# A channel-quarter pipeline for the inverse transform of a fused attention and long-convolution kernel

## The chip, the cores and the metric

The kernel runs on one core of one Trainium2 chip. The metric is the device time of one execution in microseconds (us); the kernel before takes 2488.45 us in the median of three runs (2487.83 to 2496.6). Its profiled execution spans 2488.5 us, and all instants below are counted from the start of that span.

The engines are named as the profile names them: PE (matrix multiply, with PEld for its weight loads), DVE (vector), ACT (scalar/activation), POOL and SP. SP only issues transfers here. POOL computes a little and issues transfers too. Every engine works through its own instructions in a fixed order, so an instruction that waits holds up all that stand behind it on its engine.

## The reference

Two independent results are computed and laid side by side in the output.

Part A is an attention with a recurrent memory: for each of 64 segments of 32 rows, 8 memory rows are put in front, q, k and v are formed with 1024 x 4096 weights, a masked softmax attention over 40 positions and 32 heads is taken, and the output projection gives both the segment's rows and the next memory rows. Segment s+1 needs the memory of segment s.

Part B is a long convolution (S4). In short:

```
P  = exp(dt * (A_re + i A_im) * l)              # l = 0 .. 2047, for 1024 channels x 128 states
K  = real( sum_n  C * P * dt * B )              # a filter of 2048 taps for each of 1024 channels
y  = irfft( rfft(u, 4096) * rfft(K, 4096) )[:2048] + u * Dskip
```

## The kernel before, in words

Part B comes first and takes the span up to about 811 us; part A follows, with one pass of its loop for each segment. Part A reads its weights for each segment: 17 blocks of 512 KB are streamed from DRAM for every segment (the tiles `wst`), 45 blocks are kept in SBUF ("residents"), and two in PSUM. 34 of the residents are loaded while part B still runs, by the generator `residents` (line 1279), into space that part B gives back: 4 blocks into the tile tagged `kst`, 2 into `xTl`, 4 into `wsl`, and `EARLY = 24` (line 187) into a pool of their own. The other 11 are loaded on demand in the first segment (`unit`, line 244).

Part B has these stages.

- Parameters and the cosine/sine matrix `MF` (up to about 95 us).
- Tables (about 95 to 509 us): 16 steps `f`, each for 64 channels, plus a step before and one after. The order of work is a list of words written out by hand, `ORDER` (line 590). A word such as `E3` is an exponential on ACT, `K0'` a set of matrix products that yields filter values (tile `kp`), `x0'` its eviction by DVE into `KxT` (line 900). Every fourth step, `put_values` (line 909) makes 30 stores of `KxT` into the DRAM tensor `Kd`; they are kept in the list `late` and one is issued behind each exponential (line 1004), by POOL. Words with P, U and M advance three side works: P is part A's projections for rows known in advance (`projections`, line 106: slices of weights `wsl`, results evicted into `vst` or `kst` and stored to DRAM as `PVd` and `PKd`), U is the transform of the input u (`side`, line 837: matrix products `ups` over `u_h`, sums on DVE and POOL, stored to DRAM as `Ud`), M writes transposed 128-column pieces of `MF` to DRAM as `MId` (line 824).
- Two channel halves `dh` (509 to 745 us). For each half and each of 4 frequency blocks `kc`, `pointwise` (line 1126) makes twice: the spectrum of the filter by 32 products of 512 columns into two PSUM tiles `hps` (line 1137), a copy of the odd one by ACT (`osb_`), then ten vector instructions on DVE (lines 1150 to 1163) that multiply with u's spectrum (`uq`, loaded from `Ud`, line 959) into `Bt`. The negated filter rows `KN` (line 1121) are made by ACT.
- The inverse transform (`inverse`, line 1197): 16 products of 512 columns give 128 output rows of one half (`yp`); ACT copies them to `yb`, DVE adds u times Dskip (lines 1215, 1216) and POOL issues the store (line 1217). There are 16 pieces for each half. Those of half 0 run two at a time behind each spectrum of half 1, those of half 1 run at the end (745 to 811 us), each followed by the issue of two residents from ACT's queue. Each piece first loads its matrix `mi` (256 KB, `MId`) and `uu` (a piece of u), three pieces ahead (`NIV = 3`, line 1166).

What a line can't say is the order in the last loops:

```
    for dh in range(2):
...
        for kc in range(4):
            pointwise(dh, kc, ks[dh], Bt)      # in it, after each spectrum: inverses(2 if dh == 1 else 0)
...
    for c in range(16):
        inverses(1)
        for _ in range(2):
            next(resident, None)
```

Of the kernel before, what the change touches and what calls it, by code (L numbers as in the profile page):

```python
# [64 lines left out]
class Ahead:  # L65
# [40 lines left out]
    def projections(self):  # L106
# [29 lines left out]
        for i, (m, t, c) in enumerate(slices):  # L136
# [3 lines left out]
            for j in range(2):  # L140
                a = take([128, 512], F32, "pro")
                if m == "v":
# [5 lines left out]
                    def evict(copy, a=a, t=t, c=c, j=j):  # L148
                        if late:
                            late.pop(0)()  # L150
                        vst = vals.tile([128, 2, 2, 128], BF16, name="vst", tag="vst", bufs=3)
                        copy(out=vst[:].rearrange("p b h e -> p (b h e)"), in_=a[:])
                        nc.sync.dma_start(out=self.PVd[t][:].rearrange("(b p) f -> p b f", p=128)[:, 2 * j:2 * j + 2, 256 * c:256 * c + 256],
                                          in_=vst[:].rearrange("p b h e -> p b (h e)"))
                        counted("v", t, 16, lambda: rows_out(t))
                else:
# [4 lines left out]
                    def evict(copy, a=a, m=m, t=t, g=g, h=h2 + j, mo=mo):  # L161
                        if late:
                            late.pop(0)()
# [23 lines left out]
EARLY = 24  # L187
# [409 lines left out]
def part_b(ctx, tc, u, A_re, A_im, B_re, B_im, C_re, C_im, log_dt, Dskip, out_b, ahead, copies, residents):  # L597
# [22 lines left out]
    ctx_m = ctx.enter_context(ExitStack())  # L620
    mfp = ctx_m.enter_context(tc.tile_pool(name="b_mf", bufs=1, side="right"))
    MF = mfp.tile([128, 16, 2, 512], BF16, name="MF")
# [182 lines left out]

    tmp = ctx1.enter_context(tc.tile_pool(name="b_tmp", bufs=2))
    up = ctx1.enter_context(tc.tile_pool(name="b_up", bufs=1, side="right"))
    ps_t = ctx1.enter_context(tc.tile_pool(name="b_pst", bufs=2, space=PSUM))
    ps_e = ctx1.enter_context(tc.tile_pool(name="b_pse", bufs=1, space=PSUM))
# [4 lines left out]
    def load_uh(dh):  # L814
        t_ = up.tile([128, 16, DH], BF16, name="u_h", tag="u_h")
        for r in range(4):
            sy.dma_start(out=t_[:, 4 * r:4 * r + 4, :], in_=u_r[r][:, :, DH * dh:DH * dh + DH])
        return t_[:].rearrange("p c (t s e) -> p c s t e", t=4, e=8)

# [17 lines left out]
    def side():  # L837

        for dq in range(4):
            if dq % 2 == 0:  # L840
                uv = load_uh(dq // 2)
            for kc in range(4):
                got = {}
                for r in (0, 2, 1, 3):
                    ps = take([128, 2, DQ], F32, "ups")
                    for cs in range(2):
                        for mc in range(4):
                            pe.matmul(ps[:, cs, :], lhsT=MF[:, 4 * r + mc, cs, 128 * kc:128 * kc + 128], rhs=uv[:, 4 * r + mc, 8 * (dq % 2):8 * (dq % 2) + 8],  # L848
# [25 lines left out]
    def load_par(sb):  # L874

        for q in range(2):
            for h in range(2):
                gp.dma_start(out=par_t[sb % 2][q][24 * h:24 * h + 24],
                             in_=PB[q][:].rearrange("c (d t) (g h s e) n -> d g s h c t e n", d=2, g=2, h=2, s=4)[sb // 8][sb // 4 % 2][sb % 4][h])
# [16 lines left out]
    def part_out(sb, t, kp):  # L896
        if sb % 4 == 0 and t == 0:
            KxT["t"] = tmp.tile([128, NC, 128], BF16, name="KxT", tag="KxT")
# [7 lines left out]
    def put(out, in_):  # L906
        late.append(lambda eng=gp: eng.dma_start(out=out, in_=in_))
# [51 lines left out]
    def load_u(dh, kc):  # L959
        us = {}  # L960
        for q in (0, 2, 1, 3):
            us[q] = ahead.pool.tile([128, 2, 2, DQ], F32, name="uq", tag="wsl", bufs=4)
            sy.dma_start(out=us[q][:].rearrange("p a c d -> p a (c d)"), in_=Ud[kc, 2 * dh:2 * dh + 2, :, q].rearrange("a p c d -> p a (c d)"))
        return us

# [18 lines left out]
    def phase_matmul(r, e):  # L986
        r, e = (r, e) if e else (r + 1, 0)
        pt = T["t", r, e] = ps_t.tile([128, 8 * NT], F32, name="ptt", tag="ptt")
        pe.matmul(pt[:], lhsT=pars[r][1][:, e, :], rhs=RT[:].rearrange("p a b -> p (a b)"), start=True, stop=True)
# [17 lines left out]
    def shifted(r, e):  # L1007
        kM = T["k", r, e] = tmp.tile([128, 8 * NT], F32, name="kM", tag="kM")
        sc.activation(out=kM[:], in_=T["t", r, e][:], func=ACT.Identity, bias=magic[:])

    def turns(r, e):
# [3 lines left out]
        v.scalar_tensor_tensor(out=T["n", r, e // 4][:, lo:lo + 8 * NT], in0=T.pop(("k", r, e))[:], scalar=MAGIC, in1=T.pop(("t", r, e))[:],  # L1015
# [58 lines left out]
    for f in range(-1, 17):  # L1074
# [6 lines left out]
        if f == 16:  # L1081
            while ahead.late:
                ahead.late.pop(0)()
            spectra = [load_u(0, 0)]
        for word in ORDER:
            nm, r = word.rstrip("'"), f - word.endswith("'")
            if nm in evict_of:
# [10 lines left out]
    for n_, f_ in enumerate(late):  # L1098
        f_((sy, gp)[n_ % 2])
    for g in (bg, mb):  # L1100
# [9 lines left out]
    ctx3 = ctx.enter_context(ExitStack())  # L1110
    ivs = [ctx3.enter_context(tc.tile_pool(name="b_iv", bufs=2))]
    ctx2 = ctx.enter_context(ExitStack())
    ktp = ctx2.enter_context(tc.tile_pool(name="b_KT", bufs=1))
    bp0 = ctx2.enter_context(tc.tile_pool(name="b_B0", bufs=1))
    pw = ctx2.enter_context(tc.tile_pool(name="b_pw", bufs=1))
    ps_h = ctx.enter_context(tc.tile_pool(name="b_psh", bufs=3, space=PSUM))
    ps_y = ctx.enter_context(tc.tile_pool(name="b_psy", bufs=2, space=PSUM))
    out_v = out_b.rearrange("(c p r) d -> r c p d", p=128, r=4)
    u_v = u.rearrange("(c p r) d -> r c p d", p=128, r=4)

    def negate(KT):
        KN = ahead.pool.tile([128, 8, DH], BF16, name="KN", tag="xTl")
        sc.activation(out=KN[:], in_=KT[:, 8:16, :], func=ACT.Copy, scale=-1.0)
        return KN

    def pointwise(dh, kc, KT, Bt):
        us = spectra.pop(0)
        for half in range(2):

            s_ = []  # L1130
            for r in range(2):
                ps = ps_h.tile([128, 2, DH], F32, name="hps", tag="h")
                for cs in range(2):
                    for i, rr in enumerate((r, r + 2)):
                        for mc in range(4):
                            rhs = KNs[dh][:, 4 * (rr - 2) + mc, :] if half == 1 and i == 1 else KT[:, 4 * rr + mc, :]
                            pe.matmul(ps[:, cs, :], lhsT=MF[:, 4 * rr + mc, cs, 128 * kc:128 * kc + 128], rhs=rhs,  # L1137
                                      start=(i == 0 and mc == 0), stop=(i == 1 and mc == 3))
                s_.append(ps)
            o_ = pw.tile([128, 2, DH], F32, name="osb_", tag="o")  # L1140
            if half == 0:
                sc.copy(out=o_[:], in_=s_[1][:])
            else:
                sc.copy(out=o_[:, 0, :], in_=s_[1][:, 1, :])
                sc.activation(out=o_[:, 1, :], in_=s_[1][:, 0, :], func=ACT.Copy, scale=-1.0)
            if len(KNs) == dh:
                KNs.append(negate(KT))
            qs = (0, 2) if half == 0 else (3, 1)
            X = pw.tile([128, 2, 2, DH], F32, name="x", tag="x")
            v.tensor_tensor(out=X[:, 0], in0=s_[0][:], in1=o_[:], op=ALU.add)  # L1150
            v.tensor_tensor(out=X[:, 1], in0=s_[0][:], in1=o_[:], op=ALU.subtract)  # L1151
            Y = pw.tile([128, 2, 2, DH], F32, name="y", tag="y")
            split = "p c (a d) -> p c a d"
            for n_, q in enumerate(qs):
                uc, un = (us[q][:, :, i, :].unsqueeze(1).to_broadcast([128, 2, 2, DQ]) for i in range(2))
                x_ = X[:, n_].rearrange(split, a=2)
                v.tensor_tensor(out=Y[:, n_].rearrange(split, a=2), in0=uc, in1=x_, op=ALU.mult)
                v.tensor_tensor(out=x_, in0=un, in1=x_, op=ALU.mult)
            v.tensor_tensor(out=Y[:, :, 0, :], in0=Y[:, :, 0, :], in1=X[:, :, 1, :], op=ALU.subtract)
            v.tensor_tensor(out=Y[:, :, 1, :], in0=Y[:, :, 1, :], in1=X[:, :, 0, :], op=ALU.add)  # L1160
            first = 0 if half == 0 else 1
            for j, op in ((0, ALU.add), (1, ALU.subtract)):
                v.tensor_tensor(out=Bt[:, kc, half, j], in0=Y[:, first], in1=Y[:, 1 - first], op=op)
            inverses(2 if dh == 1 else 0)

    NIV = 3

    def load_inverse(dh, c):
        r, mc = c // 4, c % 4
        iv = ivs[-1]  # L1170
        mi = iv.tile([128, 2, 4, 128], BF16, name="mi", tag="mi", bufs=NIV)
        sy.dma_start(out=mi[:], in_=MId[c])
        uu = iv.tile([128, 512], BF16, name="uu", tag="uu", bufs=NIV + 1)
        sy.dma_start(out=uu[:], in_=u_v[r, mc][:, DH * dh:DH * dh + DH])
        return mi, uu

    def negated(c, mi):
        neg = (None, (1, 2), (0, 2), (0, 1))[c // 4]
        mn = None
        if neg:  # L1180
            mn = ivs[-1].tile([128, 2, 4, 128], BF16, name="mn", tag="mn", bufs=2)
            sc.activation(out=mn[:, neg[0]:neg[1]], in_=mi[:, neg[0]:neg[1]], func=ACT.Copy, scale=-1.0)
# [4 lines left out]
    def inverses(n):  # L1187

        for _ in range(n):
            dh_, c = todo.pop(0)  # L1190
            if not ready:
                ready.append(negated(c, nxt[0][0]))
            inverse(dh_, Bs[dh_], c, *nxt.pop(0), *ready.pop(0))
# [3 lines left out]
    def inverse(dh, Bt, c, mi, uu, neg, mn):  # L1197
        r, mc = c // 4, c % 4
        iv = ivs[-1]
        yp = ps_y.tile([128, DH], F32, name="yp", tag="yp")  # L1200
        j = r % 2
        n = 0
        for kc in range(4):
# [133 lines left out]
```

## Time and profile before

| stretch (us) | what runs | PE busy | DVE busy | transfers |
|---|---|---|---|---|
| 450 to 500 | last tables | 35.07 of 50 | 44.86 of 50 | 174 GB/s |
| 500 to 550 | end of tables, half 0 | 39.10 | 36.33 | 190 GB/s |
| 550 to 600 | half 0 | 34.20 | 49.38 | 111 GB/s |
| 600 to 650 | half 0 ends, half 1 | 35.09 | 44.41 | 123 GB/s |
| 650 to 700 | half 1 with inverses | 49.09 | 40.70 | 148 GB/s |
| 700 to 750 | the same | 37.02 | 38.20 | 163 GB/s |
| 750 to 800 | last inverses, residents | 40.70 | 8.84 | 344 GB/s |
| 859 to 1300 | part A, steady | 373.10 of 441 | 232.41 of 441 | 378 GB/s |

In the profile, an engine's busy time counts instructions that compute, not those that issue transfers; PE's is a union of overlapping, pipelined products. A line of the waits reads: who waited, for whom, the total in us, how often, and the longest. In a line of a stretch the engines stand in the order PE, PEld, DVE, ACT, POOL, each with its busy time and its number of instructions, followed by PE's granted clock, the share of the transfer engines and GB/s. On the timeline a line has start, duration, engine, line, operation, output and inputs, shape, and in brackets the engine's idle time before it with what ended it.

### The profile page before, as it was taken

To read this page: it belongs to the slowest core of one execution; us is meant where nothing else is said; L and a number is where in the kernel's file an instruction comes from. 1 tells how busy PE (TensorE), PEld (TensorE's weight loads), DVE (VectorE), ACT (ScalarE), POOL (GpSimd) and SP (SyncE) were. 2 spreads that over 40 slices of the span, in tenths; PEclk is the share of its full clock that TensorE was granted. 3 is DMA by queue.
4 is the path that set the end of the run, shared out by engine and by line. 5 is a ranking of instruction groups with operands and counts; after the bars stand their busy time and mean duration, and the time that the engine had idled before them with its cause. 6 is when DMAs were issued, how large, how long until landed. Compare 5 with 4: busy or idle time off the path is not lost.

```text
span 2488.5 us, 76343 instructions
## 1 busy us (share of the span) xinstructions
PE 2017.4 (81%) x32774; PEld 1085.3 (44%) x32774; DVE 1471.0 (59%) x3159; ACT 965.1 (39%) x1543; POOL 351.7 (14%) x629
## 2 busy tenths in 40 slices
PE   1689788775978688888888888878888888888889
PEld 1356565532433244444444444444444444444444
DVE  9589788879781354545455555545555454545450
ACT  6689788911212233233333232323332323232321
POOL 2235556540001000000000000000000000000020
PEclk9799999988999799999999999999999999999999
DMA  6685964554349999999999999999999999999992
GB/s 160 180 229 157 268 185 141 157 178 138 109 153 344 358 385 383 366 378 374 378 383 387 376 389 380 385 370 351 369 388 357 386 364 383 367 383 372 382 393 81
DMA packets 383273, 763.17 MB, mean 307 GB/s; under 512 B 119462, under 2 KB 211590, under 8 KB 380886
## 3 DMA queue, kind: packets, MB, share of 16 engines
q1 hardware_dynamic: 363094, 700.46, 78.1%
q0 software_dynamic: 14928, 39.99, 4.8%
q10 hardware_dynamic: 4912, 17.84, 2.1%
q8 instruction: 256, 4.19, 0.7%
q14 instruction: 83, 0.68, 0.1%
HBM read 703.35 MB, written 67.88 MB: 310 GB/s over the span
## 4 chain that ended last, share of the span: by engine, by line
DMA 35%; PE 29%; DVE 17%; issue 10%; ACT 6%; SPq 1%; POOL 1%; DVEq 0%; ACTq 0%; POOLq 0%
DMA wst<-WD_k 16%; PE acc L339 11%; DMA wst<-WD_o 10%; PE pp L438 3%; DMA wst<-WD_v 3%; PE pe L561 2%; PE pro L158 2%; PE ups L848 2%; DVE nr L1026 2%; PE tr L350 2%; PE yp L1209 1%; DMA PVd<-vst 1%; PE pa L995 1%; DVE piece L278 1%; DMA mi<-MId 1%
## 5 line engine op out<-in xcount | busy, mean ns | idle before, releaser
L339 PEld LDWEIGHTS <-hT 128*32 128x32 bf16 x12352 | 328.1, 97 | 467.2 <-issue 247.0
L339 PE MATMUL acc<-wst,hT 128*32 128x512 bf16 x3072 | 313.3, 392 | 161.4 <-DMA wst<-WD_k 65.2
L345 ACT CAST ev<-acc 128x512 bf16<-128x512 f32 x384 | 224.7, 585 | 409.5 <-PE acc L339 404.7
L438 PEld LDWEIGHTS <-oT 128*32 128x32 bf16 x8192 | 204.2, 97 | 118.4 <-issue 92.0
L278 DVE TENSOR_SCALAR piece<-keep 128x256 int32<-128x256 int32 (+1 forms) x640 | 191.0, 363 | 53.4 <-PE pp L438 29.9
L438 PE MATMUL pp<-W_o,oT 128*32 128x256 bf16 x5120 | 211.7, 276 | 7.2 <-DMA W_o<-in_A_Wo_dram 7.2
L339 PE MATMUL acc<-W_v,hT 128*32 128x512 bf16 x3072 | 210.9, 379 | 0.0
L339 PE MATMUL acc<-W,hT 128*32 128x512 bf16 x2560 | 205.9, 393 | 0.0
L377 DVE TENSOR_REDUCE mx<-sc 128x8 f32<-128x320 f32 x128 | 62.4, 488 | 242.4 <-PE sc L370 242.2
L351 DVE COPY KT<-tr 128x512 bf16<-128x512 bf16 x64 | 27.2, 425 | 266.1 <-PE tr L350 266.1
L438 PE MATMUL pp<-wst,oT 128*32 128x256 bf16 x2560 | 128.9, 278 | 41.8 <-DMA wst<-WD_o 32.6
L358 POOL COPY KT<-pk 128x128 bf16<-128x128 bf16 x128 | 37.6, 294 | 812.2 <-PE sc L370 446.6
L351 ACT COPY QT<-tr 128x512 bf16<-128x512 bf16 x128 | 74.9, 585 | 188.5 <-PE tr L350 188.5
L1209 PE MATMUL yp<-Bt,mi 128*128 128x512 bf16 x384 | 113.3, 403 | 36.4 <-DMA mi<-MId 27.6
L425 ACT CAST oT<-pv 128x512 bf16<-128x512 f32 x128 | 75.0, 586 | 168.8 <-PE pv L411 164.7
L339 PE MATMUL acc<-W_q,hT 128*32 128x512 bf16 x1792 | 134.0, 379 | 0.0
L312 POOL COPY hT<-xt 128x192 bf16<-128x192 bf16 x64 | 22.2, 347 | 722.1 <-DMA xt<-XTd 404.7
L158 PE MATMUL pro<-xTl,wsl 128*128 128x512 bf16 x512 | 119.7, 385 | 5.2 <-ACT xTl L102 5.2
L379 ACT ACTIVATE sc<-sc 128x320 f32<-128x320 f32 x128 | 54.0, 422 | 153.8 <-DVE sc L378 150.7
L1137 PE MATMUL hps<-KT,MF 128*128 128x512 bf16 x384 | 94.1, 395 | 18.0 <-DVE x L1151 17.4
L339 PE MATMUL acc<-W_k,hT 128*32 128x512 bf16 x1536 | 108.5, 389 | 0.0
L350 PE MATMUL tr<-a_ident,ev 128*128 128x128 bf16 x1024 | 102.2, 223 | 0.8 <-ACT KT L351 0.7
(280 smaller groups left out, 3637.7 us busy)
## 6 DMA issues: line engine op xcount, KB each, us to landing
wst<-WD_o SPq DMA_DIRECT2D x320, 512.0 KB
wst<-WD_k SPq DMA_DIRECT2D x256, 512.0 KB
wst<-WD_q SPq DMA_DIRECT2D x256, 512.0 KB
wst<-WD_v SPq DMA_DIRECT2D x256, 512.0 KB
Ud<-ux POOLq DMA_DIRECT2D x16, 1024.0 KB, 5.6
uq<-Ud SPq DMA_DIRECT2D x32, 512.0 KB
pk<-PKd SPq DMA_DIRECT2D x64, 192.0 KB
wsl<-in_A_Wk_dram SPq DMA_DIRECT2D x16, 512.0 KB
```

The source lines that it names most:

```text
L158: nc.tensor.matmul(a[:], lhsT=w[:, kc, 128 * j:128 * j + 128], rhs=xTl[:, kc, :, :].rearrange("p s k -> p (s k)"), start=(kc == 0), stop=( ...
L278: nc.vector.tensor_scalar(out=out.bitcast(I32), in0=in_.bitcast(I32), scalar1=0, scalar2=None, op0=ALU.bitwise_or)
L339: nc.tensor.matmul(a[32 * g:32 * g + 32, o_:o_ + rhs.shape[1]], lhsT=hT[:, kc, :], rhs=rhs, start=(kc == 0), stop=(kc == KC - 1), tile_pos ...
L345: nc.scalar.copy(out=q[:], in_=a[:])
L350: nc.tensor.transpose(out=p[:, i, hl, :, :].rearrange("p a b -> p (a b)"), in_=q[:, 128 * hl:128 * hl + 128], identity=ident[:])
L351: eng(out=dst, in_=p[:, i, :, :, :])
L377: nc.vector.tensor_reduce(out=mx[:], in_=sc, axis=AX.X, op=ALU.max)
L379: nc.scalar.activation(out=sc, in_=sc, func=ACT.Exp, scale=scale)
L425: nc.scalar.copy(out=o[:], in_=p[:].rearrange("p a (g q) -> p a g q", g=4))
L438: nc.tensor.matmul(po[32 * qt:32 * qt + 32, :], lhsT=oT[:, h % 4, (h % 16) // 4, :], rhs=columns(w, 1024 * hh + 256 * qt, 256)[0][1], star ...
L1137: pe.matmul(ps[:, cs, :], lhsT=MF[:, 4 * rr + mc, cs, 128 * kc:128 * kc + 128], rhs=rhs, start=(i == 0 and mc == 0), stop=(i == 1 and mc = ...
L1209: pe.matmul(yp[:], lhsT=m_[:, cs, kc, :], rhs=Bt[:, kc, half, j, c_, :], start=(n == 0), stop=(n == 15))
```

## The change: four channel quarters in one pipeline

The transform is cut into 16 blocks: four channel quarters of 256 channels, four frequency blocks each. A block's spectrum covers both halves of the complex result at once (64 products of 256 columns), and is issued one block ahead of its pointwise part, so that the next spectrum stands on PE before the inverses. From block 4 on, each block is followed by two inverse groups of the previous quarter (a group is two pieces of 128 rows, 32 products of 256 columns), and 8 groups are left for the end. The inverse matrices are loaded once and kept in SBUF (`MI`, 32 KB for each partition) instead of being read for each half. The first block's spectrum goes into the PSUM tiles of the tables' own pools and is issued at the start of the tables' last step; its `KN` is made by POOL at the end of the step before that. The order of the channels in the tables is changed to fit (`load_par`).

Around it: the 30 stores of each `put_values` are issued by SP instead of POOL; two stores of the list `late` of the projections, not one, go with each eviction, and `vst` has 6 buffers, not 3; `u_h` is loaded in quarters into two buffers, the second and third well ahead; the last such stores (`PKd` from `PVd`) are issued after the filter stores; `uu` comes through POOL's queue, in one transfer for two pieces; the residents are issued by SP, in other places (3 at block 0, 4 at block 6, 8 at block 14 into the space of `MF`, 19 with the last inverses).

```diff
-                        if late:
+                        for _ in range(min(2, len(late))):
                             late.pop(0)()
-                        vst = vals.tile([128, 2, 2, 128], BF16, name="vst", tag="vst", bufs=3)
+                        vst = vals.tile([128, 2, 2, 128], BF16, name="vst", tag="vst", bufs=6)
...
-EARLY = 24
+EARLY = (3, 13)
...
-    def load_uh(dh):
-        t_ = up.tile([128, 16, DH], BF16, name="u_h", tag="u_h")
+    def load_uq(dq):
+        t_ = up.tile([128, 16, DQ], BF16, name="u_h", tag="u_h%d" % (dq % 2))
...
     def put(out, in_):
-        late.append(lambda eng=gp: eng.dma_start(out=out, in_=in_))
+        late.append(lambda eng=sy: eng.dma_start(out=out, in_=in_))
...
         if f == 16:
-            while ahead.late:
-                ahead.late.pop(0)()
-            spectra = [load_u(0, 0)]
+            spectra = [load_u(0), load_u(1)]
         for word in ORDER:
+            if f == 15 and word == "u0":
+                negate(ks[0], gp)
+            if f == 16 and word == ORDER[0]:
...
+                spectrum(0, first)
...
     for n_, f_ in enumerate(late):
         f_((sy, gp)[n_ % 2])
+    while ahead.late:
+        ahead.late.pop(0)()
...
+    for b in range(16):
...
+        if b == 0:
+            ks.append(load_k(1, (gp,), ktp.tile([128, 16, DH], BF16, name="KT", tag="KT")))
+            for _ in range(EARLY[0]):
+                next(resident)
+        if b == 3:
+            nxt = [load_inverse(*todo[n_]) for n_ in range(NIV)]
+            pointwise(b, *now)
...
+        if b + 1 < 16:
+            s_ = [ps_h.tile([128, 2, 2, DQ], F32, name="hps", tag="h") for _ in range(2)]
+            spectrum(b + 1, [halves(t_) for t_ in s_])
+            then = s_[0][:], odd([halves(t_) for t_ in s_])
+        if b == 6:
+            negate(ks[1])
+            for _ in range(4):
+                next(resident)
+        if b == 14:
+            for _ in range(8):
+                next(resident)
+        if b != 3:
+            pointwise(b, *now)
+        now = then
+        if b + 2 < 16:
+            spectra.append(load_u(b + 2))
+        if b < 4:
+            sy.dma_start(out=MI[:, 4 * b:4 * b + 4], in_=MId[4 * b:4 * b + 4].rearrange("c p a k q -> p c a k q"))
+        if b >= 4:
+            inverses(2)
     ctx2.close()
-    ctx_m.close()
-    for c in range(16):
+    for _ in range(8):
         inverses(1)
-        for _ in range(2):
+        for _ in range(3):
             next(resident, None)
```

## The prediction

> **What bounds the kernel now.** I read the slices of the span first. Part A (right of the 14th slice) has its transfers at 0.9 or more throughout; the stretches in the table above give 378 GB/s at share 1.00 there. The change leaves its 17 streamed blocks per segment alone, so what part A takes after its first segment (859 to 2488 us) stays. All that can move is part B.
>
> ```profile
> ## 2 busy tenths in 40 slices
> PE   1689788775978688888888888878888888888889
> DVE  9589788879781354545455555545555454545450
> ACT  6689788911212233233333232323332323232321
> ...
> DMA  6685964554349999999999999999999999999992
> ```
>
> Each digit stands for 62.2 us. In slices 3 to 8, most of the tables, DVE and ACT are both at 0.7 to 0.9. Then DVE alone is high, then PE, then transfers: three stages that follow one another with one busy engine each. That is what a pipeline could fold together. Next the waits of three stretches. Tables, 95 to 512 us:
>
> ```profile
> ACT vst L152 <- DMA PVd<-vst: 12.8, 4, 4.5
> DVE kst L167 <- DMA PVd<-vst: 8.7, 2, 4.6
> ACT kst L167 <- DMA PVd<-vst: 4.5, 2, 2.6
> PEld L848 <- DMA u_h<-in_B_u_dram: 2.2, 1, 2.2
> ```
>
> ACT and DVE stop for a store of `vst` to land, since only three buffers exist. How much this costs I read from the timeline: the first of each step's two DVE instructions of line 1026 that the chain lists comes 23.0 us after that of the step before in undisturbed steps, but steps that evict `vst` or change `u_h` take 26 to 29. Summed over the steps from 120.86 to 497.16 us, the excess over 23.0 us is 31.5 us.
>
> Half 0 and half 1:
>
> ```profile
> DVE x L1150 <- DMA Kd<-KxT: 10.7, 1, 10.7
> ...
> PE hps L1137 <- DVE x L1151: 17.4, 5, 4.8
> ```
>
> ```profile
> ACT yb L1214 <- PE yp L1209: 47.3, 20, 11.1
> DVE uu L1216 <- ACT yb L1214: 42.6, 14, 4.9
> ...
> PE yp L1209 <- DMA mi<-MId: 27.6, 7, 14.9
> ```
>
> DVE idles 10.7 us between its last table eviction (509.37) and the first `x` (520.07), because PE, ACT and DVE start the first spectrum only then; the named store is merely the last of several releasers. Until 616 us PE waits for DVE and no inverse runs. At the end PE waits for `mi` while residents fill the queues. So 509.4 to 811.0 us (DVE's last add, 810.58 + 0.42), 301.6 us, is the stretch to rework.
>
> [...] the trace has 1214 to 1226. The new pointwise keeps ten instructions of 1024 elements per partition, so it must cost the same. [...] 8 products `ups` of 256 columns take 1.03 us, (1.03 - 0.27)/7 = 0.109 us each, weight loads hidden. [...] The trace shows what issue costs: 18 filter stores on SP took 13.71 us (0.76 each), on POOL 8 took 4.53 (0.57).
>
> **The change, part by part.**
>
> Tables. More `vst` buffers, two `late` stores per eviction and `u_h` in two buffers aim at the 31.5 us. Six evictions fit a 23 us step, so a buffer comes round after a whole step; the `vst` waits seen were under 5 us beyond three buffers, so they go. Not all the excess need go: `kst` still has one buffer. Against it, 90 filter stores of the first three quarters move to SP inside the tables: 90 x 0.76 = 68 us of issue over 370 us, in front of `wsl` loads that are issued three slices (one step) ahead. SP has gaps (it issues nothing from 163 to 172 us, for one), so I count this as hidden. Bounds 0 and -31; I take -20.
>
> POOL's `KN`. 4096 bf16 per partition; from POOL's copies of 128 and 192 elements (294, 347 ns) 0.83 ns per element, 3.6 us in all. Behind it stand the last `ux` sums (7.2 us) and `Ud` store, needed only by the last quarter. `KT` has been loaded by 491 + 2 us, so `KN` is ready by about 498, and the first spectrum (64 x 0.109 = 7.0 us) ends by 502, before the last `kp` products (505.7). ACT is free from 500.7. Hence DVE starts the first `x` right after its last table cast: -10.7.
>
> Blocks 0 to 3. DVE: 11.85 us per block (532.69 to 544.54, one old half-block without a gap), 47.4 in all. PE needs 7 of each 12. One new wait: SP has 15 filter stores (11.5 us), 8 `PKd` stores (8 x 1.33 from 10.68 for 8), `Dsk` and three residents in front of the load for block 2. That is issued about 25 us after the tables' end, and behind 1.6 MB of residents and scattered stores lands at about 34, while DVE wants it at 26: +8 (0 to 15). Nothing else stands behind it but DVE itself.
>
> Blocks 4 to 15. DVE: 11.85 + 4 adds of u in 1.90 (645.16 to 647.06) = 13.75. PE: 64 + 64 products x 0.109 = 13.95. ACT: odd copies, `yb`, negated matrices, under 7. With the spectrum one block ahead, PE and DVE need not wait for each other within a block: the even tile of block b is freed by DVE's `x` two spectra later. So 11 blocks at 13.9 (153), the last pointwise 11.85, then 8 groups x 3.49 = 27.9 and 1.5 to evict: 194. `KN` for the second half (3.62 us on ACT) and `MI` (4.2 MB, once, where 8.4 MB were read) lie beside DVE's work.
>
> Sum: 47.4 + 8 + 194 = 250 us from the tables' end, against 301.6: -52, the 10.7 included.
>
> Hand-over. The residents no longer have 66 us of tail. 8 can go once the last spectrum is done, 12 groups (42 us) before the end, 19 more by the end: 27 x 0.524 = 14.2 MB, with u and the outputs 17.3 MB, at 344 to 378 GB/s 46 to 50 us, so 4 to 8 us late. The two blocks for PSUM, formerly fetched at 732 us, now wait for space until the inverses are over: before, PE resumed 8.6 us after its last inverse; a chain of store, load, copy and load makes about 12. The two overlap in part: +5 (0 to 12). The first segment then loads its 28 blocks as before (811 to 859).
>
> Total: 2488.5 - 20 - 52 + 5 = 2421.5, say 2422.
>
> **Rivals.**
>
> - Tables gain nothing: SP's new work eats what the buffers give. For it: SP holds to its order, and waits up to 10.9 us for `vst` producers in single cases. Against: POOL loses as much. 2488.5 - 52 + 5 = 2441.
> - PE and DVE in lockstep from block 4: if the next spectrum had to wait for this block's `x`, a block would be x 2.45 + the rest of the spectrum 5.2 + inverses 7.0 + ACT 0.75 + DVE 0.43 = 15.8; 11 x 1.9 = 21 more: 2443. For it: three double-bank PSUM tiles serve two per block. Against: the odd tile is free as soon as ACT has copied it.
> - Everything better: -31 in the tables, no stall at block 2 (-60 in place of -52), no late loads: 2488.5 - 31 - 60 = 2397.5. For it: PE's tail leaves slack that I gave to neither. Against: the residents' 46 us of transfers in 42.
> - Slower: SP becomes the bound of the tables, and the 68 us of issue lie on the path, with the rest as forecast: 2488.5 + 68 - 52 + 5 = 2509. For it: part A's projections depend on SP's loads. Against: issue is idle for whole stretches.
>
> **How the numbers follow.** Forecast 0.52, tables gain nothing 0.20, lockstep 0.13, better 0.09, slower 0.06. Range: 2398 to 2460. The low end is the better case. The high end is no gain in the tables (+20), a stall 7 us longer and a hand-over 7 us later together (2456), or lockstep with one of these (2450). Outside are the slower case, part of the better one and lockstep without the tables' gain (2463): about 2 in 10. Faster by over 0.5% (under 2476): 0.93; within: 0.03; slower: 0.04.
>
> **What would show it.** Tables: waits for `PVd` gone, steps of 23 us, end near 490. Start: first `x` within 1 us of the last table cast. Blocks: `x` every 12, then every 14 us; a wait of DVE for `uq` at block 2. PE at 9 tenths from block 4 on. `mi` waits gone. First segment's PE about 10 to 14 us after the last inverse. Part A's steady part unchanged at 1629 us. Wrong it would be if SP's queue holds up `wsl`, if blocks take 16 us, or if the residents are later than 10 us.

## The result, and the profile after

The changed kernel takes 2430.78 us (median of 4 runs, 2426.8 to 2432.11) against 2488.14 us before on the same chip (4 runs, 2483.58 to 2496.6). The ratio is 0.9763, with a 95% interval from 0.9734 to 0.9792. The forecast was 2422 us within 2398 to 2460. The profiled execution spans 2428.7 us, 59.8 us less than before.

Cut at instants that both timelines show, the 59.8 us are made up as follows (a step begins at DVE's first sign-bit clearing, line 1026 before, 1050 after; the tables end with the last cast into `KxT`; the transform ends with DVE's last addition to `uu`; the third segment of part A is dated by its copy of `KT`, line 351).

| stretch | before (us) | after (us) | difference | forecast |
|---|---|---|---|---|
| to the start of the tables' last step | 494.87 | 462.51 | -32.4 | |
| last step, to the tables' end | 14.5 | 25.1 | +10.6 | both: -20 |
| tables' end to the transform's end | 301.6 | 254.7 | -46.9 | -52 |
| transform's end to the third segment | 77.0 | 85.0 | +8.0 | +5 |
| the rest of part A | 1600.5 | 1601.4 | +0.9 | 0 |

The slices of the span come first, as before; a digit now stands for 60.7 us.

```profile
PE   1699999669996888888888888888888888888879
...
DVE  9599999989972445455554545454545545454540
ACT  6699999603332233232333333332323233332321
...
DMA  6686974583368999999999999999999999999992
```

PE, DVE and ACT stand together at 9 in slices 3 to 7, where before they changed between 7 and 9. In slices 10 to 12 PE and DVE are high at once (9, 9, 9 and 9, 9, 7), where before DVE was high first and PE later. Between the two, in slices 8 and 9 (425 to 546 us), PE has 6: there the last step and the first blocks lie. A table of stretches says the same in busy time: the columns are the ends of the stretch, its length, the busy time of PE, PEld, DVE, ACT and POOL (with counts), PE's granted clock, the share of the transfer engines and GB/s.

```profile
500.00:550.00 50.00, 31.29 (x233) 25.37 (x234) 40.43 (x36) 3.41 (x9) 19.27 (x34) 0.76 0.90 292
550.00:600.00 50.00, 47.06 (x432) 41.89 (x431) 44.74 (x47) 19.76 (x33) 8.68 (x12) 1.00 0.45 158
600.00:650.00 50.00, 50.00 (x461) 44.79 (x459) 47.12 (x52) 14.65 (x29) 11.56 (x16) 1.00 0.32 107
650.00:700.00 50.00, 50.00 (x461) 44.77 (x459) 47.66 (x50) 16.55 (x32) 8.67 (x12) 1.00 0.39 131
```

From 600 to 700 us PE is busy for the whole of both stretches and DVE for 47 of 50: the pipeline is bound by PE, one block each 13.97 us. What is lost against the forecast up to the transform's end lies before 600 us. Three of the waits between 455 and 545 us name most of it (who waited, for whom, total, times, longest):

```profile
...
ACT nr L1053 <- DVE nr L1050: 9.5, 2, 7.9
...
DVE y L1167 <- DMA uq<-Ud: 7.6, 1, 7.6
PE pa L989 <- POOL KN L974: 6.3, 1, 6.3
```

The second line is the stall at block 2 that was forecast at 8. The first and the third were not forecast. DVE's timeline shows what stands behind the first, and POOL's what stands behind both:

```profile
460.69 0.63 DVE L1039 SCALAR_TENSOR_TENSOR nr<-kM,ptt 128x464 f32<-128x464 f32 x1
...
461.58 0.63 DVE L1039 SCALAR_TENSOR_TENSOR nr<-kM,ptt 128x464 f32<-128x464 f32 x1
462.12 0.43 DVE L902 CAST KxT<-kp 128x264 bf16<-128x264 f32 x1
462.51 9.44 DVE L1050 TENSOR_SCALAR nr<-nr 128x1856 int32<-128x1856 int32 x1
471.87 1.42 DVE L1057 TENSOR_SCALAR wn<-sn 128x768 bf16<-128x768 bf16 x1
473.21 2.19 DVE L1050 TENSOR_SCALAR nr<-nr 128x1856 int32<-128x1856 int32 x1
```

```profile
460.40 10.57 POOL L974 TENSOR_SCALAR KN<-KT 128x4096 bf16<-128x4096 bf16 x1 [1.27 <-DMA PVd<-vst]
470.96 2.11 POOL L866 TENSOR_TENSOR ux<-us 128x512 f32<-128x512 f32 x1
```

Line 1050 took 1.6 us in every step before this one. Here it takes 9.44 us without any idle time ahead of it, and it ends within 1 us of POOL's negation. DVE counts as busy in this time, so no list of DVE's waits shows it; it shows only in the duration of a single row, and in ACT, which waits for that row. So the theory to be tested was that POOL's `KN` shuts DVE out ("the lock" below: a name for what these rows show; what makes it in the chip no run shows). The two rows of line 1039 above, with one input from PSUM (`ptt`), ran beside the negation at their ordinary 0.63 us.

### The profile page after: what moved, and what is told of

Read it like the earlier page. It is cut to its first block, busy times and chain, and to the rows that moved or that the text cites. A ratio compares the mean times of both kernels' runs of the same rounds, so it can differ in the third digit from the quotient of the medians.

```text
span 2428.7 us, 78387 instructions
## 1 busy us (share of the span) xinstructions
PE 2009.3 (83%) x33798; PEld 1184.6 (49%) x33798; DVE 1480.1 (61%) x3159; ACT 976.1 (40%) x1598; POOL 345.6 (14%) x578
## 4 chain that ended last, share of the span: by engine, by line
DMA 34%; PE 26%; DVE 9%; issue 6%; ACT 3%; SPq 1%; POOL 1%; ACTq 0%; DVEq 0%; POOLq 0%
DMA wst<-WD_k 15%; PE acc L339 13%; DMA wst<-WD_o 12%; PE pp L438 3%; DMA wst<-WD_v 2%; PE pe L561 2%; PE tr L350 2%; DMA out_dram<-uu 2%; DMA wst<-WD_q 2%; DVE piece L278 2%; ACT ev L345 1%; PE hps L989 1%; DMA W_o<-in_A_Wo_dram 1%; PE yp L1216 1%; DVE ob L527 1%
## 5 line engine op out<-in xcount | busy, mean ns | idle before, releaser
L339 PE MATMUL acc<-W,hT 128*32 128x512 bf16 x4608 | 366.2, 388 | 0.0
L989 PEld LDWEIGHTS <-MF 128*128 128x128 bf16 x1024 | 104.4, 102 | 44.3 <-issue 24.3
L1216 PE MATMUL yp<-Bt,MI 128*128 128x256 bf16 x768 | 114.9, 276 | 3.6 <-DVE Bt L1173 3.6
L989 PE MATMUL hps<-KT,MF 128*128 128x256 bf16 x720 | 95.7, 286 | 20.6 <-DVE x L1163 17.5
L350 PEld LDWEIGHTS <-ev 128*128 128x128 bf16 x1024 | 58.4, 98 | 98.2 <-issue 67.9
```

The lines of the kernel that those rows point to most:

```text
L339: nc.tensor.matmul(a[32 * g:32 * g + 32, o_:o_ + rhs.shape[1]], lhsT=hT[:, kc, :], rhs=rhs, start=(kc == 0), stop=(kc == KC - 1), tile_pos ...
L350: nc.tensor.transpose(out=p[:, i, hl, :, :].rearrange("p a b -> p (a b)"), in_=q[:, 128 * hl:128 * hl + 128], identity=ident[:])
L989: pe.matmul(s_[r][half][:, cs, :], lhsT=MF[:, 4 * rr + mc, cs, 128 * kc:128 * kc + 128], rhs=rhs, start=(i == 0 and mc == 0), stop=(i == 1 ...
L1216: pe.matmul(yp[:, b, :], lhsT=m_[:, b, cs, kc, :], rhs=Bt[:, kc, j, half, c_, :], start=(n == 0), stop=(n == 15), skip_group_check=True)
```

## Experiments

All are variations of the changed kernel, unless it is said that they are of the kernel before. The texts of what was expected call DVE VectorE, ACT ScalarE, POOL GpSimd and SP SyncE. Times are medians; ratios are to the kernel before on the same chip, and since the kernels ran on more than one chip, whole times are compared by their ratios. From the third to the last segment part A runs the same instructions in each of these kernels, and this stretch took from 1503.5 to 1518.8 us in the 14 profiled executions. Differences of a few us are therefore read from the stages of the trace and not from the whole.

| kernel | time (us) | ratio, interval | tables' end | transform's end | third segment |
|---|---|---|---|---|---|
| changed | 2430.78 | 0.9763 (0.9734 to 0.9792) | 487.63 | 742.3 | 827.3 |
| first `KN` on DVE | 2417.37 | 0.9714 (0.9688 to 0.9741) | 477.6 | 730.8 | 813.7 |
| second `KN` on POOL | 2427.57 | 0.9751 (0.9724 to 0.9778) | 487.0 | 744.2 | 828.8 |
| `PKd` stores later | 2416.33 | 0.9713 (0.9686 to 0.9739) | 486.7 | 733.7 | 816.7 |
| first spectrum late | 2410.39 | 0.9691 (0.9669 to 0.9713) | 476.2 | 733.5 | 819.2 |
| three `vst` | 2444.23 | 0.9812 (0.9781 to 0.9843) | 504.4 | 761.8 | 846.6 |
| one late store | 2444.01 | 0.983 (0.9804 to 0.9855) | 509.8 | 762.7 | 845.4 |
| `Kd` stores on POOL | 2426.76 | 0.9752 (0.9729 to 0.9775) | 490.0 | 743.7 | 828.4 |
| before, with two of the table edits | 2473.45 | 0.9945 (0.993 to 0.9961) | 496.1 | 796.3 | 875.1 |
| transform alone | 2456.61 | 0.9875 (0.9836 to 0.9913) | 518.2 | 773.4 | 858.0 |
| matrices from DRAM | 2437.52 | 0.9804 (0.9761 to 0.9846) | 487.5 | 742.1 | 828.4 |
| three repairs | 2403.61 | 0.9672 (0.9649 to 0.9695) | 476.8 | 723.4 | 808.8 |
| three repairs, second `KN` moved | 2407.85 | 0.9673 (0.9631 to 0.9715) | 477.3 | 720.6 | 805.0 |

### The first negation on DVE

```diff
-            if f == 15 and word == "u0":
-                negate(ks[0], gp)
...
             if f == 16 and word == ORDER[0]:
+                negate(ks[0], v)
```

> First negation KN on VectorE ahead of the last step's first sign-bit clearing (L1050), instead of on GpSimd. Theory: GpSimd's 10.57 us KN shuts VectorE out, so that L1050 took 9.44 us; then L1050 is back at 1.6 us, L1057 at 0.9, the KN takes about 2.5 us on VectorE, PE's 6.3 us wait in the first spectrum shrinks to 1 to 3, and the last step (from 462.5 to the tables' end) takes 16.5 to 18 us instead of 25.1: 7 to 9 us less in all. Rival: L1050 is slow because of PE's spectrum or of the loads that run beside it, or the sine order of ScalarE sets the last step anyway; then L1050 stays above 5 us or the tables end at 487 again, and the time is within 2 us of the changed kernel.

The tables ended at 477.6, 10.0 us earlier. DVE's timeline at the same place:

```profile
462.67 1.49 DVE L974 TENSOR_SCALAR KN<-KT 128x4096 bf16<-128x4096 bf16 x1 [0.86 <-DMA PVd<-vst]
464.08 1.64 DVE L1050 TENSOR_SCALAR nr<-nr 128x1856 int32<-128x1856 int32 x1
465.64 0.88 DVE L1057 TENSOR_SCALAR wn<-sn 128x768 bf16<-128x768 bf16 x1
```

Lines 1050 and 1057 are back at what they take in the other steps, and the whole negation costs DVE 1.49 us where POOL took 10.57. The rival (something else slows line 1050) is out: the spectrum and the loads still run beside it. Block 2 still stalls, by 6.2 us.

Two kernels further down say the same from another side. In them POOL began its negation a little later, and line 1050 took only 1.13 us; the next row of DVE that met the lock stood instead. With the `Kd` stores on POOL this was line 1057:

```profile
462.90 1.13 DVE L1050 TENSOR_SCALAR nr<-nr 128x1856 int32<-128x1856 int32 x1
463.94 10.71 DVE L1057 TENSOR_SCALAR wn<-sn 128x768 bf16<-128x768 bf16 x1
```

```profile
463.79 10.65 POOL L974 TENSOR_SCALAR KN<-KT 128x4096 bf16<-128x4096 bf16 x1 [3.64 <-DMA KT<-Kd]
```

With one late store it was line 1001, a product of two inputs, at 9.75 us.

### The second negation on POOL

```diff
         if b == 6:
-            negate(ks[1])
+            negate(ks[1], gp)
```

> The second negation KN (of the second half's kernel values) on GpSimd instead of ScalarE. Theory A (GpSimd shuts VectorE out only of those forms that the tables use, one input, and KN takes some 10 us on GpSimd by itself): KN 9 to 10.6 us here too, VectorE's two-input operations in that block keep their durations within 10%, the block of 17.1 us goes back to 14.0, 3 us less in all. Theory B (any VectorE operation is shut out): some VectorE operation near 580 us grows by 5 us or more and the block is no shorter, or longer: 0 to 6 us more. Theory C (KN's 10.57 us was itself mostly waiting for VectorE's lock): KN takes under 6 us here.

Here DVE runs only instructions with two inputs. DVE's rows, then POOL's:

```profile
577.95 1.23 DVE L1168 TENSOR_TENSOR x<-uq,x 128x1024 f32<-128x1024 f32 x1
579.21 9.72 DVE L1170 TENSOR_TENSOR y<-y,x 128x1024 f32<-128x1024 f32 x1
588.85 1.21 DVE L1171 TENSOR_TENSOR y<-y,x 128x1024 f32<-128x1024 f32 x1
```

```profile
578.06 11.52 POOL L974 TENSOR_SCALAR KN<-KT 128x4096 bf16<-128x4096 bf16 x1 [3.65 <-PE hps L989]
```

Theory B holds for the rows that came up here. ("Any" operation goes too far: line 1039 ran on under the first negation.) The instruction under way is finished (577.95 + 1.23 = 579.18), and the next one stands until POOL is done (579.21 + 9.72 = 588.93, against 589.58). If POOL got no further until DVE's row was over, its 11.52 us contain about 1.1 us of waiting, and 10.4 remain. The same 10.4 remain in the two kernels named above (10.65 less 0.24 with the `Kd` stores on POOL, 11.37 less 0.97 with one late store), so I take this, an estimate from the three rows, for what POOL needs with DVE standing, for 4096 elements per partition. Theory C (under 6 us) is out. The block took 22.4 us from one `x` to the next, instead of 17.1, but the blocks after it took 13.6 instead of 13.97: DVE was now the later one and ran at its own pace, and the transform ended only 1.9 us later. The time (2427.57) doesn't tell this from no difference.

### Eight stores behind two loads

```diff
-    while ahead.late:
-        ahead.late.pop(0)()
     for g in (bg, mb):
...
             spectra.append(load_u(b + 2))
+        while b == 1 and ahead.late:
+            ahead.late.pop(0)()
```

> The last eight PKd stores (9.6 us of issue on SyncE just after the tables) issued behind the spectra loads of block 3 instead of ahead of block 2's. Theory: SyncE's issue order makes the loads of block 2's spectra late; then the stall at block 2 (7.6 us) vanishes or falls below 1 us and the whole is 6 to 8 us shorter. Rival: the loads are late because of the bytes moved at that time (KT, MI, the residents); then the stall stays above 4 us and the gain is under 3 us.

In the changed kernel SP issues these after the tables:

```profile
487.66 8.56 SPq L909 DMA_DIRECT2D Kd<-KxT  x15
496.27 9.59 SPq L124 DMA_DIRECT2D PKd<-PVd  x8
505.90 1.48 SPq L1141 DMA_DIRECT2D Dsk<-in_B_Dskip_dram  x1
508.19 1.42 SPq L193 DMA_DIRECT2D W_k<-in_A_Wk_dram  x3
509.70 1.58 SPq L965 DMA_DIRECT2D uq<-Ud  x2
```

With the stores moved the last line, the load for block 2, stands at 497.88 and the wait is gone; blocks 2 and 3 begin 11.84 us apart:

```profile
511.23 1.22 DVE L1160 TENSOR_TENSOR x<-hps,osb__7415 128x1024 f32<-128x1024 f32 x1
512.36 1.22 DVE L1161 TENSOR_TENSOR x<-hps,osb__7415 128x1024 f32<-128x1024 f32 x1
523.07 1.22 DVE L1160 TENSOR_TENSOR x<-hps,osb__7510 128x1024 f32<-128x1024 f32 x1
```

So the stall is one of issue order. From the tables' end to the transform's end it is now 247.0 us instead of 254.7, which is the 7.6 us of the wait.

### Nothing of the transform beside the last step

```diff
-            if f == 15 and word == "u0":
-                negate(ks[0], gp)
-            if f == 16 and word == ORDER[0]:
-                s0 = ps_e.tile([128, 2, 512], F32, name="pa", tag="pa")
...
-                spectrum(0, first)
...
+    negate(ks[0], v)
+    s0 = ps_e.tile([128, 2, 512], F32, name="pa", tag="pa")
...
+    spectrum(0, first)
     for n_, f_ in enumerate(late):
```

> The first block's negation and spectrum are put behind the last table operations (negation on VectorE), so nothing of the transform lies beside the last step. Theory: the advance of the first spectrum (10.7 us before against 0.8 after) was paid back by GpSimd's 10.57 us lock in the last step; so the tables end 10 to 11 us earlier, the first x comes 9 to 12 us after them, that is within 2 us of the changed kernel's, and the whole is within 3 us of it. Rival: the lock is only partly what lengthened the last step; then the tables' end moves by less than 6 us and the whole is 4 to 8 us longer.

The tables ended 11.4 us earlier and the first `x` came 9.2 us after them, at 485.45; this is 3.0 us earlier than with the advance, where the theory allowed 2. What the theory missed is block 2: blocks 2 and 3 now stand 11.84 us apart. In the changed kernel the spectra for block 2 arrive 34.6 us after the tables' end (DVE's row behind the wait starts at 522.28), and with the first `KN` on DVE 33 us after it. A transform that starts 9 us later meets them in time. The advance of the first spectrum was thus given back twice over, 10 us by POOL's negation and what would have remained by the wait for these loads. The transform ended 8.9 us earlier than the changed kernel's. By the ratios the whole is about 18 us shorter. Of this the third segment shows 8.1; the rest lies in part A, whose stretch from the third to the last segment took some 10 us less in this execution (1505.5 against 1515.8), and no run assigns that to the edit.

### What brought the tables' 32 us

Three kernels, each with one edit undone: three `vst` buffers, one late store at an eviction, `Kd` stores on POOL's queue.

```diff
-tag="vst", bufs=6
+tag="vst", bufs=3
```
```diff
-                        for _ in range(min(2, len(late))):
+                        if late:
```
```diff
-        late.append(lambda eng=sy: eng.dma_start(out=out, in_=in_))
+        late.append(lambda eng=gp: eng.dma_start(out=out, in_=in_))
```

> Only the six buffers of vst go back to three. Theory: the buffers are what removes VectorE's and ScalarE's waits for the PVd stores in the tables; then these waits come back, about 20 to 32 us of steps (23.0 each without them) return, and the whole is 15 to 32 us longer. Rival: popping two late stores at an eviction, or the Kd stores' move from GpSimd's to SyncE's queue, is what removed them; then the table steps stay at 23.0 and the time is within 5 us of the changed kernel.

> Only the number of late stores issued at an eviction goes back from two to one; six buffers of vst stay. Theory: the buffers did the work, the pops nothing: table steps stay at 23.0 us, the tables end within 2 us of the changed kernel's, and the time is within 4 us. Rival: with one pop the queue of late stores is not worked off in time, waits on vst or on the stores come back or the stores left at the end delay the loads behind them: 5 to 15 us longer.

> Only the Kd stores go back to GpSimd's queue. Theory: on SyncE's queue they compete with the PVd and PKd stores and add issue time there; on GpSimd they stand in front of its side work, which has slack in the table steps, so steps stay near 23.0 and the time is within 4 us of the changed kernel. Rival 1: GpSimd's waits for KxT delay its parameter loads and side work, as before the change, and steps grow: 5 to 12 us longer. Rival 2: SyncE is relieved of 0.6 us a store before the KT loads and the spectra, and block 2's stall falls: 3 to 8 us shorter.

With three buffers the last step began at 479.20, 16.7 us later; three steps took 28 us or more, and the waits on `vst` stood in the list again:

```profile
ACT vst L152 <- DMA PVd<-vst: 15.2, 4, 5.0
```

This is the theory's mechanism, a little under the 20 to 32 us that it gave the steps; the third segment came 19.3 us later. With one late store my theory fell: the last step began at 484.10, 21.6 us later, with three steps of 29.1 to 30.7 us, because the evictions into `kst` waited for stores that were still in the list:

```profile
ACT kst L167 <- DMA PVd<-vst: 6.1, 2, 3.7
DVE kst L167 <- DMA PVd<-vst: 5.8, 1, 5.8
...
DVE kst L167 <- DMA PKd<-kst: 4.5, 1, 4.5
ACT kst L167 <- DMA PKd<-kst: 2.5, 1, 2.5
```

With the `Kd` stores on POOL the steps stayed at 23.0 us and the last one began at 462.90; the tables ended 2.4 us and the transform 1.4 us later than in the changed kernel. That move was worth 2 us at most.

Then the other way round: the kernel before, with six buffers and two late stores and nothing else (the first two of these diffs, read from below).

> The kernel before with six buffers of vst and two late stores at an eviction, and nothing else of the change. Theory: these two made the tables' 32.4 us by themselves (each alone, undone, gives back 17 to 22); so all steps take 23.0 us, the last step begins at 462 to 464 instead of 494.9, it takes 14.5 us as it has no lock, the tables end at 477 to 479, and the whole is 2454 to 2460. Rival: the Kd stores on SyncE or u's quarters have a part; then some steps stay at 26 us and the last step begins after 470.

The rival holds. Of the 15 steps before the last one 14 took 23.0 to 23.4 us, and one took 41.1 us. In it PE stood still, as its row on the timeline shows:

```profile
274.32 1.03 PE L848 MATMUL ups<-u_h,MF 128*128 128x256 bf16 x8
299.52 1.89 PE L848 MATMUL ups<-u_h,MF 128*128 128x256 bf16 x8 [18.00 <-DMA u_h<-in_B_u_dram]
```

`u_h` has one buffer there; SP issued the load of its second half at 289.89, behind eight `PKd` stores. So the last step began at 481.62, 13.3 us earlier than before, not 32. Undone alone, the buffers and the late stores cost 17 and 22 us; put in together they bring 13. The 18.0 us of this wait are close to what is missing, so the quarters of `u_h` with two buffers are the likely third part of the gain. No kernel undoes them alone; that they are it is read from this one wait.

### The transform alone

The three edits of the last section (`vst`, late stores, `Kd` stores) together, on the changed kernel.

> The changed kernel with three buffers of vst, one late store at an eviction and the Kd stores on GpSimd's queue, as before; the pipeline over quarters stays. Theory: the tables' last step begins at 493 to 497 again and takes 25 us with GpSimd's lock (tables' end 518 to 522, 10 later than before), the transform from there takes 250 to 256 us instead of 301.6, the hand-over 6 more: 28 to 34 us less than before, 2454 to 2460. Rival: without the tables' gain the loads of the spectra come relatively earlier (more of the late stores are done by then), block 2's stall goes, and the transform takes 245 to 248: 2446 to 2452.

The last step began at 493.07, only 1.8 us earlier than before, though `u_h` still comes in quarters: these too bring little without the six buffers and the second late store. It ended at 518.2, and from there the transform took 255.1 us. The theory holds, with the stall at block 2, so the rival is out:

```profile
DVE y L1167 <- DMA uq<-Ud: 8.0, 1, 8.0
PE pa L989 <- POOL KN L974: 6.4, 1, 6.4
```

### Inverse matrices from DRAM

```diff
+        mi = iv.tile([128, 2, 2, 4, 128], BF16, name="mi", tag="mi", bufs=NIV + 1)
+        sy.dma_start(out=mi[:], in_=MId[c:c + 2].rearrange("c p a k q -> p c a k q"))
...
-                    for half, m_, c_ in ((0, MI[:, c:c + 2], cs), (1, mn[:] if minus else MI[:, c:c + 2], g_cs)):
+                    for half, m_, c_ in ((0, mi[:], cs), (1, mn[:] if minus else mi[:], g_cs)):
```

> The inverse matrices are loaded for each group of two pieces from DRAM again (512 KB each, five groups ahead, on SyncE's queue) instead of once into SBUF; 16.8 MB are read instead of 4.2. Theory: within blocks 4 to 15 transfers are at a third of what they can do and the loads stay hidden, so blocks stay at 14 us; at the end the last loads and the residents share the queue, the last 8 groups or the hand-over grow: 5 to 12 us longer in all, none of it before block 14. Rival: SyncE's order (a spectrum's load waits for its buffer, an inverse's load behind it) stops PE earlier: blocks of 15 us and more, 15 to 40 us longer.

Blocks kept their 13.97 us, the transform ended at 742.1 (742.3 in the changed kernel) and the third segment came 1.1 us later. The stretch from 600 to 690 us shows why:

```profile
600.00:690.00 90.00, 90.00 (x827) 80.67 (x826) 84.92 (x93) 26.48 (x54) 19.53 (x27) 1.00 0.59 193
```

The transfer engines have a share of 0.59 where it was 0.33, and PE doesn't notice. Neither forecast fits: keeping the matrices in SBUF is worth about 1 us here, and the intervals of the two ratios overlap. No engine waits for `mi` in this kernel, where PE waited 27.6 us for it before. So it is not the place in SBUF that took this wait away; loading five groups ahead and the new places of the residents are left, and no run parts them.

### The three repairs together

Both negations on DVE, the `PKd` stores behind the loads for block 3, and the three early weight tiles behind those for block 4. Beside the first and the third diff of this section:

```diff
         if b == 0:
...
-            for _ in range(EARLY[0]):
-                next(resident)
...
         if b == 6:
-            negate(ks[1])
+            negate(ks[1], v)
...
+        if b == 2:
+            for _ in range(EARLY[0]):
+                next(resident)
```

> Both negations KN on VectorE, the eight PKd stores behind the spectra loads of block 3 and the three early weight tiles behind those of block 4. Theory: the three repairs lie in stretches that don't overlap and add up: 10.0 (tables' end, measured with the first KN moved), 8.6 (block 2's stall, measured with the stores moved) and 2 to 3 (the 3.0 us that ScalarE's second KN put into its block, less what VectorE's 1.5 us cost there), together 20 to 22 us less than the changed kernel, about 2409. Rival: what follows is bound elsewhere (the weights' loads up to the hand-over, which take their time whenever the transform ends); then the gain found at the tables and at block 2 shrinks at the hand-over and the total is under 15 us, above 2415.

The transform ended at 723.4 and the third segment came 18.5 us earlier than in the changed kernel, close to the 20 to 22 forecast (by the ratios it is about 23 us in all, with part A's scatter in it). The gains add up, and the hand-over does not take them back. The second negation went wrong, though: put ahead of block 6's `x`, DVE waited there for PE to have read the first `KN`, whose buffer it takes.

```profile
559.64 1.23 DVE L974 TENSOR_SCALAR KN<-KT 128x4096 bf16<-128x4096 bf16 x1 [5.87 <-PE hps L989]
```

Blocks 5 and 6 stood 21.1 us apart. The last kernel moves this one instruction:

```diff
         if b != 3:
             pointwise(b, *now)
+        if b == 6:
+            negate(ks[1], v)
```

> As the kernel with the three repairs, but the second KN stands on VectorE behind the pointwise part of block 6 instead of ahead of it. Theory: ahead of it, VectorE stood 5.9 us until PE had read the first KN (one buffer), which ended the pipeline's lead; behind it that wait is over before VectorE comes there, block 5 to 6 takes 14 us instead of 21.1, and blocks run at PE's 14.0 us; against 13.6 where VectorE catches up, the transform ends 3 to 5 us earlier and the whole is 2399 to 2401. Rival: that wait was only a shift that the later blocks (13.57 us) absorbed; then the end of the transform moves by under 1.5 us.

```profile
566.18 1.22 DVE L974 TENSOR_SCALAR KN<-KT 128x4096 bf16<-128x4096 bf16 x1
```

No wait stands ahead of it, blocks 5 and 6 are 13.97 us apart and 6 and 7 14.71. The 7.1 us by which they stood further apart in the kernel above are the wait and the row itself (5.87 + 1.23): all that came after it in DVE's order stood too. The transform ended 2.8 us earlier still and the third segment came 3.8 us earlier, about what the theory asked. The whole time did not follow (ratios 0.9673 and 0.9672), and part A from the third to the last segment took 1518.8 us in this kernel's profiled execution and 1503.5 in the other's. The repaired kernels are faster than both the changed kernel and the one before; which of the two is the faster in total is not settled.

## Why the prediction was right, and where it was not

**Tables, -20.** Measured -21.7, but as the difference of two terms that I had otherwise; that the sum came so near is luck. The waits went altogether: -32.4, a little beyond my better bound of -31, with each step at 23.0 us. I gave a third of this away for `kst`'s single buffer and SP's issue time, and neither mattered: the second late store keeps `kst` free, and the `Kd` stores matter by 2 us at most on either queue. Then the last step gave 10.6 back.

**POOL's `KN`: the step that failed.** The prediction put it at "3.6 us in all", taken from POOL's copies at 0.83 ns per element, and found it hidden, as only POOL's own work was queued behind it. It took 10.57 us, 2.6 ns per element, and what it held up stood on another engine. The row to go by was POOL's sum of two inputs, `ux` of 512 elements, at 1.27 us and more (2.5 ns per element). The copies' rate holds for copies (294 ns for 128 elements and 1040 for 1024 in the trace before), but not for this row, though it too has one input (DVE does it in 1.22 to 1.49 us). The lock was not asked about at all; in the trace after, DVE's blocked row ends within 1 us of POOL's (471.95 against 470.97).

**First `x`, -10.7.** It came 0.8 us after the tables' end, as said. But the instant it is counted from had moved by 10, and the loads for block 2 cancel the rest: with the first spectrum late the transform ended 8.9 us sooner. As built, the advance is worth less than nothing; with the negation on DVE and the stores later the first `x` comes 8 us sooner (477.53 in the kernel with the three repairs against 485.45) and no stall follows. What that is worth at the transform's end was not measured: no kernel has the first spectrum late and the stores later.

**Blocks 0 to 3, 47.4 + 8.** Measured 56.8, of which the stall is 7.6 (a pointwise row of 1024 elements took 1.21 to 1.23 us, as in the trace before); 1.4 more is a wait of block 4's `x` for ACT's copy of its spectrum, which the sum left out. The issue order in front of the loads was read rightly (the wait ended 34.6 us after the tables' end, 34 forecast), and moving eight stores proved it.

**Blocks 4 to 15 and the tail, 194.** Measured 197.1. A block takes 13.97 us (13.95 by PE's 128 products at 0.109 us), so PE does not wait for DVE. The three us over are the second `KN`, costed at nothing as it would "lie beside DVE's work":

```profile
579.96 3.64 ACT L976 ACTIVATE KN<-KT 128x4096 bf16<-128x4096 bf16 x1
583.48 1.92 ACT L1188 ACTIVATE mn<-MI 128x2048 bf16<-128x2048 bf16 x1
```

It did lie beside DVE's work, but on ACT a negated matrix `mn` stood behind it, for which PE waited 2.9 us. That block took 17.1 us.

**`MI` in SBUF.** Counted at nothing beyond the pipeline, and found to be worth about 1 us. The waits for `mi` went, as forecast, but they go without it too.

**Hand-over, +5.** Measured +8.0 to the third segment. PE resumes 13.8 us after its last inverse (8.6 before); in between, transfers run at 149 GB/s, and the first segment then loads at 386:

```profile
742.00:755.00 13.00, 0.41 (x12) 0.38 (x16) 4.41 (x11) 0.00 (x0) 2.71 (x11) 0.59 0.45 149
755.00:800.00 45.00, 31.56 (x459) 14.03 (x462) 13.04 (x36) 8.84 (x16) 0.93 (x3) 0.69 1.02 386
```

That fits the chain of store, load, copy and load that I described; the 12 us that I gave it were an estimate with no row of the trace behind it. It was not tested by a kernel of its own; the runs show only that it stays at 83 to 86 us when the transform ends up to 22 us earlier.

**Part A.** Its steady part was put at no change, and shows none beyond its scatter.

By the traces the kernel gained 59.8 us of 67 forecast. The 7 us between are 10.6 for the lock, 5.1 in the transform, 3 in the hand-over and 0.9 in part A, less 12.4 that the tables gave beyond my estimate. The rivals are answered too. The tables gained; there was no lockstep; SP's queue did not bound the tables, but it did bound block 2.

## What to carry to other kernels

A small instruction moved to an idle engine is not free because that engine is idle: look beside it for single rows of other engines that have grown (here one from 1.6 to 9.44 us), since the time lost counted as busy and stood in no list of that engine's waits. When work is started earlier, follow what it will need next. Here it ran into loads whose arrival was fixed by the order of one queue, and starting earlier gained nothing until eight stores were moved. Where several waits stand in the same steps, undoing one edit shows what it is worth with the others in place, and putting in only some of them shows less; here only both directions told that the two edits I had named were not enough.

## What the runs showed of the hardware

- Negating 128 x 4096 bf16 took 1.22 to 1.49 us on DVE, 3.64 on ACT and 10.57 to 11.52 on POOL, while POOL's copies took 0.83 ns for each further element (294 ns for 128, 347 for 192, 1040 for 1024).
- During that row on POOL, DVE finished the instruction under way, and the next one that the lock met stood for the rest: 9.44 us for a 128x1856 int32 operation of one input that takes 1.13 with POOL at rest, 10.71 us for a 128x768 bf16 one of one input that takes about 0.35, 9.72 us for a 128x1024 f32 operation of two SBUF inputs that takes 1.22. The two rows with one input from PSUM and one from SBUF that came up in the changed kernel went on (line 1039, 0.63 us each).
- A milder form stood in every step: beside POOL's `ux` sums line 1050 took 1.54 to 1.65 us and line 1057 0.88, and with POOL at rest 1.13 (the two kernels in which the negation began later) and about 0.35. Right behind the lock line 1050 took 2.19. No run takes the sums away from POOL, so what this costs the steps is open.
- From the third to the last segment the same instructions took 1503.5 to 1518.8 us in 14 executions, with the transfer engines at a share of 1.00 or 1.01 from 860 to 2180 us in each. This scatter hides what a stage gains or loses below some 10 us.
